# The first 25 microseconds of a grouped-query attention backward: K's load first, q and grad_out by ACT's queue, zero matmuls and an early exponential

## The chip, the cores and the metric

The kernel runs on one core of one Trainium2 chip. The metric is the device time in microseconds; the time before is the median of three runs. One further execution is taken with the hardware profiler, and all views of the profile come from it.

## The reference

Attention with 32 query heads on 4 key/value heads, 4 query positions and 2048 keys, for 32 batches, all in bf16; the kernel returns the output and the gradients of q, k and v for a given grad_out.

```python
B, Hq, Hkv, Sq, Sk, D = 32, 32, 4, 4, 2048, 128
k = jnp.repeat(k, rep, axis=1)
v = jnp.repeat(v, rep, axis=1)
scores = jnp.einsum("bhqd,bhkd->bhqk", q, k) * D ** -0.5
p = softmax(scores)
out = jnp.einsum("bhqk,bhkd->bhqd", p, v)
_out, _vjp = jax.vjp(forward, q, k, v)
return (_out, *_vjp(grad_out))
```

## The kernel before

A batch has 32 x 4 = 128 query rows, one for each partition, 32 for each key/value head. Its K and V are 2 MB each and lie in SBUF as 128 partitions x 4 heads x 16 chunks x 128; a load is four transfers, one for each head (lines 153 and 159), issued by SP. K has three buffers, V two. q and grad_out of four batches come together, by two transfers in GROUP (line 141): 128 partitions x 4 batches x 128 elements, so in runs of 256 bytes. Batch 0's pair is issued by SP inside LK(0), ahead of K; the later pairs are issued by POOL.

The work of a batch is cut into pieces with short names. QDT transposes q and grad_out on PE into one PSUM bank, and DVE copies both to SBUF as qdt (lines 170 and 172). KT0 to KT7 and VT0 to VT7 (function turned) each transpose eight 128 x 128 blocks of K or V on PE (line 180) and have DVE copy the bank (line 182); a piece with an even number needs heads 0 and 1, one with an odd number heads 2 and 3. Sa and Sb are the two halves of the scores: Sa needs KT0 to KT3, Sb KT4 to KT7, both need qdt; DVE takes the maximum of each (line 210) and forms negb (line 213). EXa and EXb are ACT's exponentials (line 221). NRM adds the two row sums (ls, line 236), takes the reciprocal, and POOL scales grad_out and q by it (line 230) into block pairs dop and qp, which are set to zero at the start (line 117). ETa and ETb transpose the exponentials back, O is the output, dP the gradient of the scores (line 349), dST its transpose, dQ, dV and dK the results; dV and dK are cast from PSUM by ACT (line 310) and stored by POOL (line 132), in the tail by SP.

The order in which every engine gets its instructions is written out by hand: HEAD names the pieces of the first iterations ("KT4@0" is piece KT4 of batch 0), STEADY those of one iteration, TAIL those of the last. Each engine runs its share of that order one after the other, and a piece that waits holds up what stands behind it on its engine. PSUM's eight banks are given out by the class Banks in the same order: the bank or pair that has been free longest. Both the scores' halves take two banks, a transposed piece one.

## Time and profile before

| | |
|---|---|
| runs, device us | 685.06, 686.15, 687.32 (median 686.15) |
| the profiled execution: its own time / its span | 682.75 / 680.5 us |
| busy share of the span | PE 92%, PEld 66%, DVE 87%, ACT 83%, POOL 38% |
| moved by transfers | 274.45 MB, mean 403 GB/s |
| granted clock of TensorE | 0.998 |
| K quarter loads, issue to landing, median | 14.5 us |

A busy share is an average over the whole span. PE is matrix work, PEld the loading of its weights, which overlaps; DVE, ACT and POOL are the other compute engines; SPq stands for SP's queue of transfer issues. In the views by time, a row has its start, its length, the engine, the line and the tiles, and in brackets how long the engine was idle before it and what it waited for. In the table by stretches, each engine's busy time in that stretch is followed by its number of instructions; the last three columns are the granted clock, the mean busy share of the 16 transfer engines, and what they moved in GB/s. A wait for several marks is put down in the profile to the one that came last, and where that one had long been there, it was another.

### The profile page before, as it was taken

What the parts mean: (1) busy time and instruction counts of PE and PEld (TensorE: products, weight loads), DVE (VectorE), ACT (ScalarE), POOL (GpSimd) and SP (SyncE); (2) the same over time, 40 slices, a digit from 0 to 9 for tenths busy, and PEclk for the clock granted to TensorE, in tenths of its full rate; (3) what the DMA queues carried; (4) which work ended last, traced back from release to release, by engine and by line L of the source; (5) the groups of instructions that cost most, each with busy time, mean ns of one, the idle gap of its engine ahead of it and who ended that gap; (6) DMA issues with size and microseconds to landing.
All of it is one profiled execution on the core that took longest, in us unless ns stands there. A gap on an engine that the chain in (4) does not pass through costs nothing.

```text
span 680.5 us, 27999 instructions
## 1 busy us (share of the span) xinstructions
PE 623.7 (92%) x12352; PEld 449.1 (66%) x12352; DVE 594.5 (87%) x1003; ACT 563.3 (83%) x666; POOL 259.6 (38%) x436
## 2 busy tenths in 40 slices
PE   5899999999999999988999999899999999899984
PEld 4577766667776667765667766577666677566652
DVE  4999999899899889889888889789898898898895
ACT  0599898898888888888988888888888888896885
POOL 1254243534424454432535324353244542344310
PEclk9999999999999999999999999999999999999999
DMA  8989999999999999999999999999999999999998
GB/s 326 406 293 400 416 417 411 416 413 416 416 414 417 412 417 415 416 416 415 416 416 414 416 414 417 414 411 416 414 417 398 409 414 416 415 401 406 370 368 317
DMA packets 76483, 274.45 MB, mean 403 GB/s; under 512 B 8579, under 2 KB 8651, under 8 KB 76361
## 3 DMA queue, kind: packets, MB, share of 16 engines
q1 hardware_dynamic: 42185, 145.11, 53.2%
q0 software_dynamic: 34176, 127.55, 46.6%
q8 instruction: 96, 1.57, 0.8%
q14 instruction: 26, 0.21, 0.1%
HBM read 136.31 MB, written 136.31 MB: 401 GB/s over the span
## 4 chain that ended last, share of the span: by engine, by line
PE 53%; DMA 36%; DVE 4%; ACT 3%; issue 2%; SPq 1%; POOL 0%; ACTq 0%; DVEq 0%; POOLq 0%
DMA k_sb<-in_k_dram 35%; PE banks L180 22%; PE banks L306 14%; PE banks L263 8%; PE banks L197 5%; PE banks L247 5%; ACT dv L310 2%; DVE kt L182 1%; DMA v_sb<-in_v_dram 1%; SPq L153 1%; DVE dk L310 1%; DVE m L210 1%; PE banks L170 1%; DVE ds L349 1%; DVE vt L182 0%
## 5 line engine op out<-in xcount | busy, mean ns | idle before, releaser
L310 ACT CAST dv<-banks 128x1024 bf16<-128x1024 f32 x254 | 244.4, 1025 | 47.7 <-PE banks L306 47.1
L310 ACT CAST dk<-banks 128x1024 bf16<-128x1024 f32 x251 | 246.0, 1022 | 29.9 <-PE banks L306 26.9
L182 DVE COPY kt<-banks 128x1024 bf16<-128x1024 bf16 x256 | 165.1, 680 | 9.9 <-PE banks L180 9.8
L182 DVE COPY vt<-banks 128x1024 bf16<-128x1024 bf16 x256 | 166.4, 680 | 2.6 <-PE banks L180 2.0
L180 PE MATMUL banks<-ident,k_sb 128*128 128x128 bf16 x2048 | 148.0, 221 | 18.5 <-DMA k_sb<-in_k_dram 13.3
L230 POOL TENSOR_SCALAR dop<-do_sb,rinv 32x128 bf16<-32x128 bf16 x124 | 74.2, 598 | 220.6 <-PE banks L306 125.2
L180 PE MATMUL banks<-ident,v_sb 128*128 128x128 bf16 x2048 | 143.5, 219 | 12.4 <-ACT dv L310 8.8
L180 PEld LDWEIGHTS <-k_sb 128*128 128x128 bf16 x2048 | 120.7, 99 | 48.4 <-issue 31.8
L180 PEld LDWEIGHTS <-v_sb 128*128 128x128 bf16 x2048 | 121.3, 98 | 28.2 <-issue 26.2
L306 PE MATMUL banks<-dop,e 64*128 64x256 bf16 x1024 | 97.6, 273 | 7.0 <-issue 4.3
L349 DVE SCALAR_TENSOR_TENSOR ds<-banks,delta,e 128x1024 bf16<-128x1024 f32 x64 | 82.0, 1283 | 17.1 <-PE banks L197 17.0
L306 PE MATMUL banks<-qp,ds 64*128 64x256 bf16 x1024 | 87.0, 272 | 2.6 <-DVE dk L310 1.1
L132 POOL DMA_DIRECT2D out_dram<-dv x46 | 32.5, 708 | 139.9 <-ACT dv L310 133.5
L230 POOL TENSOR_SCALAR qp<-q_sb,srinv 32x128 bf16<-32x128 bf16 x128 | 77.9, 609 | 10.7
L221 ACT ACTIVATE e<-banks,negb 128x1024 bf16<-128x1024 f32 x64 | 70.7, 1111 | 11.4 <-DVE negb L213 11.4
L210 DVE TENSOR_REDUCE m<-banks 128x1 f32<-128x1024 f32 x64 | 75.2, 1215 | 1.7 <-PE banks L197 1.5
L306 PEld LDWEIGHTS <-e 64*128 64x128 bf16 x1024 | 34.0, 94 | 52.9 <-issue 36.6
L249 DVE COPY et<-banks 128x1024 bf16<-128x1024 bf16 x64 | 41.4, 685 | 27.1 <-PE banks L247 27.0
L306 PEld LDWEIGHTS <-ds 64*128 64x128 bf16 x1024 | 40.8, 94 | 30.8 <-ACT dv L310 12.6
L249 DVE COPY dst<-banks 128x1024 bf16<-128x1024 bf16 x64 | 43.4, 679 | 0.0
L197 PE MATMUL banks<-vt,qdt 128*32 128x512 bf16 x512 | 41.3, 384 | 1.8 <-issue 1.6
L197 PE MATMUL banks<-kt,qdt 128*32 128x512 bf16 x512 | 39.6, 384 | 0.7 <-DVE vt L182 0.3
(40 smaller groups left out, 460.1 us busy)
## 6 DMA issues: line engine op xcount, KB each, us to landing
k_sb<-in_k_dram SPq DMA_DIRECT2D x128, 512.0 KB, 14.5
v_sb<-in_v_dram SPq DMA_DIRECT2D x128, 512.0 KB, 20.5
out_dram<-dk POOLq DMA_DIRECT2D x29, 2048.0 KB, 23.4
out_dram<-dv POOLq DMA_DIRECT2D x22, 2048.0 KB, 27.5
out_dram<-dv POOLq DMA_DIRECT2D x7, 1440.0 KB, 27.2
out_dram<-dk SPq DMA_DIRECT2D x2, 2048.0 KB, 10.3
out_dram<-dv POOLq DMA_DIRECT2D x7, 512.0 KB, 20.4
out_dram<-dv SPq DMA_DIRECT2D x1, 2048.0 KB, 12.0
```

Of the source, the lines that this page charges most:

```text
L180: nc.tensor.transpose(out=ps[:, 4 * hh + j, :], in_=S[which][:, 2 * (i % 2) + hh, 4 * (i // 2) + j, :], identity=ident[:])
L182: nc.vector.tensor_copy(out=S[f"{which}t{i}"][:], in_=ps)
L197: nc.tensor.matmul(ps[G * h:G * h + G, a, :], lhsT=S["qdt"][:, col, G * h:G * h + G], rhs=xt[:, 4 * (h % 2):4 * (h % 2) + 4, :].rearrange( ...
L210: nc.vector.reduce_max(out=S["m"][:, i:i + 1], in_=S[f"s{i}"][1], axis=AX.X)
L221: nc.scalar.activation(out=S[f"e{i}"][:], in_=ps, func=ACT.Exp, bias=S["negb"][:], scale=scale, accum_out=S["l"][:, i:i + 1],)
L230: engine.tensor_scalar(out=t[r, h % 2, :], in0=src[r, :], scalar1=by[r, :], scalar2=None, op0=ALU.mult)
L247: nc.tensor.transpose(out=ps[:, u, :], in_=S[f"{src}{i}"][:, P * u:P * u + P], identity=ident[:])
L249: nc.vector.tensor_copy(out=S[f"{name}{i}"][:], in_=ps)
L263: nc.tensor.matmul(ps[G * h:G * h + G, :], lhsT=S[f"{xt}{c // 8}"][:, c % 8, G * h:G * h + G], rhs=S[kv][:, h, c, :], start=(c == 0), stop ...
L306: nc.tensor.matmul(ps[:, a, :, c, :], lhsT=S[f"{x}{i // 4}"][r, u:u + P], rhs=S[y][r, :, :], start=True, stop=True, tile_position=(2 * G * ...
L310: copy(out=S[name][:, :, 2 * i:2 * i + 2, :].rearrange("p h c d -> p h (c d)"), in_=banks.ap(t).rearrange("p a (j w) -> p (a j) w", j=2),)
L349: nc.vector.scalar_tensor_tensor(out=S[f"ds{i}"][:], in0=ps, scalar=S["delta"][:], in1=S[f"e{i}"][:], op0=ALU.subtract, op1=ALU.mult,)
```

## The change

Batch 0's q and grad_out are issued by ACT in place of SP, so that SP's first transfer is K's first quarter. Behind these two issues, ACT takes one exponential of a single column of the identity, and with it the load of the exponential's table. On PE, 16 matrix products of the identity with the zeroed pair dop (256 columns, into one bank that is given back unread) stand ahead of everything else. Batch 0's pieces get another order: KT4 stands ahead of QDT, KT1 ahead of KT5 and KT7, and VT2 behind Sa and Sb. KT5 and KT7 of batch 0 are copied out of PSUM by ACT in place of DVE.

```diff
 HEAD = """
-LK@0 LV@0 QDT@0 KT4@0 KT6@0 KT2@0 KT0@0 KT3@0 KT5@0 KT1@0 KT7@0 LK@1 LV@1 VT2@0 Sa@0 Sb@0 VT5@0 VT3@0 EXb@0 VT4@0 EXa@0 VT0@0 QDT@1 KT4@1
+LK@0 LV@0 WARM@0 KT4@0 QDT@0 KT6@0 KT2@0 KT0@0 KT3@0 KT1@0 KT5a@0 KT7a@0 LK@1 LV@1 Sa@0 Sb@0 VT2@0 VT5@0 VT3@0 EXb@0 VT4@0 EXa@0 VT0@0 QDT@1 KT4@1
...
+WARM_MATMULS = 16
...
         if b == 0:
-            GROUP(0, nc.sync)
+            GROUP(0, nc.scalar)
+
+            first = sm_pool.tile([P, 1], FP32, name="first")
+            nc.scalar.activation(out=first[:], in_=ident[:, 0:1], func=ACT.Exp)
...
+    def WARM(b):
+
+        t = banks.take(1)
+        for _ in range(WARM_MATMULS):
+            nc.tensor.matmul(
+                banks.ap(t)[:, 0, 0:2 * D], lhsT=ident[:], rhs=pairs["dop", 0][:].rearrange("p a d -> p (a d)"), start=True, stop=True,
+            )
+        banks.give(t)
+
-    def turned(S, which, pool, i):
+    def turned(S, which, pool, i, copy=nc.vector.tensor_copy):
...
-        nc.vector.tensor_copy(out=S[f"{which}t{i}"][:], in_=ps)
+        copy(out=S[f"{which}t{i}"][:], in_=ps)
...
-    def KT(b, i):
-        turned(st[b], "k", kt_pool, i)
+    def KT(b, i, copy=nc.vector.tensor_copy):
+        turned(st[b], "k", kt_pool, i, copy)
...
+        table[f"KT{i}a"] = lambda b, i=i: KT(b, i, nc.scalar.copy)
```

More of the change, by code (lines that the diff above doesn't have):

```diff
@@ L352, in dP @@
         banks.give(t)
-    table = {"LK": LK, "LV": LV, "QDT": QDT, "O": O, "dQ": dQ, "NRM": NRM}
+    table = {"LK": LK, "LV": LV, "QDT": QDT, "O": O, "dQ": dQ, "NRM": NRM, "WARM": WARM}
     for i, c in enumerate("ab"):
```

## The prediction

> **What bounds the kernel now.** I read the whole-run bandwidth first, then the chain of waits, then a table by stretches of the first 65 us, then the first 25 us in order of time.

> ```profile
> span 680.5 us, 27999 instructions
> GB/s 326 406 293 400 416 417 411 416 413 416 416 414 417 412 417 415 416 416 415 416 416 414 416 414 417 414 411 416 414 417 398 409 414 416 415 401 406 370 368 317
> PE 53%; DMA 36%; DVE 4%; ACT 3%; issue 2%; SPq 1%; POOL 0%; ACTq 0%; DVEq 0%; POOLq 0%
> ```

> Each slice is 17 us. From the fourth to the thirty-seventh the transfers move some 415 GB/s almost without a break, and 274.45 MB at that rate are 661 of the 680.5 us: the run is a transfer stream with a poor start and a compute tail. The chain puts 53% on PE and only 36% on DMA, but the PE share lies before 260 us, where the engines are nearly full as well; the rate says that the stream has no room to catch up. The first and the third slice are what a head edit can touch. Stretch by stretch (us; busy time of PE, PEld, DVE, ACT, POOL; clock; DMA share; GB/s):

> ```profile
> 15.00:20.00 5.00, 3.38 (x51) 2.57 (x44) 4.96 (x8) 1.86 (x2) 0.00 (x0) 1.00 1.02 405
> 32.00:34.00 2.00, 2.00 (x32) 0.90 (x31) 2.00 (x4) 2.00 (x4) 0.00 (x0) 1.00 1.03 416
> 34.00:36.00 2.00, 1.49 (x28) 1.10 (x21) 1.96 (x3) 1.97 (x3) 0.64 (x1) 1.00 0.57 225
> 42.00:44.00 2.00, 2.00 (x42) 1.73 (x35) 1.18 (x4) 1.95 (x4) 1.17 (x2) 1.00 0.75 211
> 58.00:60.00 2.00, 1.99 (x33) 1.76 (x32) 2.00 (x5) 1.54 (x3) 0.00 (x0) 1.00 1.03 422
> ```

> Until 34 us the stream is full with the loads of batches 0 to 2. Then it runs at half rate until about 48 us, because what comes next waits for compute: the first dv store is issued at 35.36 us, K of batch 3 at 42.13, V of batch 3 at 47.23. Summed over 34 to 54 us, 5.98 MB move where 415 GB/s would move 8.3: 5.6 us of stream time are lost. So what makes batch 0's compute earlier or later by x moves these issues by x, and the end with them, since the stream is full behind them.

> The head in order of time (start, length, engine):

> ```profile
> 0.73 0.42 SPq L141 DMA_DIRECT2D q_sb<-in_q_dram  x1
> 1.75 1.92 SPq L153 DMA_DIRECT2D k_sb<-in_k_dram  x4
> 4.33 0.29 PE L170 MATMUL banks<-ident,do_sb 128*128 128x128 bf16 x1 [0.97 <-DMA do_sb<-in_grad_out_dram]
> 8.31 5.60 PE L180 MATMUL banks<-ident,k_sb 128*128 128x128 bf16 x60 [0.66 <-DMA k_sb<-in_k_dram]
> 9.81 0.69 DVE L182 COPY kt<-banks 128x1024 bf16<-128x1024 bf16 x1 [0.16 <-PE banks L180]
> 15.98 1.74 PE L180 MATMUL banks<-ident,v_sb 128*128 128x128 bf16 x28 [0.22 <-DMA v_sb<-in_v_dram]
> 17.96 2.47 DVE L182 COPY vt<-banks 128x1024 bf16<-128x1024 bf16 x4
> 18.13 1.28 ACT L221 ACT_TABLE_LOAD   x1 [18.13 <-DVE negb L213]
> 23.20 0.15 DVE L236 TENSOR_TENSOR ls<-l 128x1 f32<-128x1 f32 x1
> ```

> q and grad_out are in by 4.33, K's second quarter by 8.30, V's last quarter by 15.98. DVE works nearly without a gap from 8.95 to 23.20, where it has the row sums (ls); POOL then scales grad_out and dV can start. I use the start of ls as the head's mark: the chain of waits goes through it.

> **The parts of the change and their cost.**

> K first. The first 256-byte packet of q starts at 2.06 us, the first K packet at 3.25, so K starts about 1.2 us earlier. Gain at K's second quarter, before other effects: 1.2 us.

> q and grad_out on ACT's queue. They are 1024 packets of 256 B in the trace, 64 for each of 16 transfer engines at 18 ns; K and V are 1024 packets of 4096 B, also 64 for each engine, at 159 ns. Before, one queue held them in a row. Now two queues are full together, and what matters is how an engine shares itself. The trace has one stretch for this: from 54 to 56 us, POOL's stores and SP's loads both waiting, 102 and 103 packets of 4096 B were started. That is turn for turn, but equal sizes can't tell turns by packet from turns by bytes. By bytes, 256 KB land beside the first 256 KB of K, by about 5 us. By packets, grad_out's last packet has turn 64, together with V's last: 15.98 - 1.2 + 64 x 0.018 = 15.9 us. If ACT's issue is 0.42 us ahead of SP's (one issue, row above), 22 of its packets pass alone and the last has turn 42: V's second quarter less a little, 11.9 us. The nearest row for a small load beside a full queue is POOL's:

> ```profile
> v_sb<-in_v_dram SPq DMA_DIRECT2D x128, 512.0 KB, 20.5
> q_sb<-in_q_dram POOLq DMA_DIRECT2D x7, 128.0 KB, 22.9
> q_sb<-in_q_dram SPq DMA_DIRECT2D x1, 128.0 KB, 2.3
> ```

> Alone it takes 2.3 us, beside others no less than a load four times its size (some of it behind stores in its own queue). That is nearer to turns by packet; I take the middle of 11.9 and 15.9, so 13.9.

> [...]

> Order. QDT of batch 0 now stands behind KT4 and ahead of the seven other K pieces on PE, whose instructions run in order, and it needs grad_out. KT4 is done at about 7.8; then KT6 to KT7, the scores, and on DVE everything from the qdt copy on, wait for 13.9 where QDT waited only to 4.33 before. From grad_out's landing: 0.29 for two transposes, four pieces at the pace of a PE that has idled (DVE got the first at 8.95, 9.81, 10.66: 0.85 each) 3.4, then KT3 and KT1 leave DVE at 5.1. ACT takes KT5 and KT7 behind that: its copy of a bf16 bank is not in the trace, between DVE's 0.69 and the exponential's 1.11; I take the f32 cast's 1.02, so 6.7. Sb 0.6, its maximum 1.17, negb 0.2: 8.7. Then five V pieces (VT2 now stands behind the maxima) at 0.68, qdt 0.28, four K pieces of batch 1 2.72: ls at 15.2 behind the landing, 29.1 us, against 23.20: **+5.9**. At 11.9 it is +3.9, at 15.9 +7.9; it breaks even at 8.0.

> Zero matmuls: 16 of 256 columns. At 0.106 for 128 columns (0.85 for eight) 3.4 us, at L306's 273 ns 4.4; from the identity's 1.55 they end by 6.0, ahead of K's second quarter (8.30 - 1.2 + 16 x 0.018 = 7.4). They cost nothing while K is that late. What they could win is the 0.16 of each cold piece, at most 5 x 0.16 = 0.8; with PE idle from 7.8 to 13.9 I take none. [...]

> One exponential ahead: the table load's 1.28 goes to ACT's idle time before 18 us. It is off the path: from negb to ls DVE has 6.4 us of copies, the two exponentials take 2.3. Bounds: 0, and -1.28 if they led. I take 0. KT5 and KT7 on ACT take 2 x 0.69 from DVE; that is in the sum.

> Transfers behind: the build's waits have K of batch 1 wait for grad_out's completion mark, so SP issues it at 13.9 and not at 7.01. Its loads have 1 to 3 us of idle stream behind V, but batch 1's K is needed only at 24 or later, and the gap from 34 us covers the rest.

> **Sum.** 682.75 (the profiled execution's own time) + 5.9 = 688.7. The runs' median, 686.15, is 3.4 above that execution; on it the forecast is **692.0**, its own range 690.0 to 694.1.

> **Rivals.**
> 1. Shared by bytes, the far side: grad_out lands by 5, no stall. K pieces leave DVE by 12.3, negb is there at 15.4. But V's last quarter still lands at 15.98, since as many bytes go ahead of it; then four V pieces, qdt, four K pieces: 16.6 + 2.7 + 0.3 + 2.7 = 22.3, -0.9: 685.2. For it: nothing but the lack of a row with unequal packets. Against: POOL's row.
> 2. No stall, and the exponential leads, not DVE: it starts at 15.5 and not at 19.42, -3.9: 682.2. For it: PE waited 0.8 us for an exponential's bank. Against: DVE's 4.96 busy of 5.00.
> 3. A half stall: the landing at 8 to 9, as if ACT's queue had most of its packets ahead: 0 to +1, 686.7. Against: both engines leave the same barrier, and SP's first issue is at 0.73.

> **Chances.** Forecast 0.54, rival 1 0.17, rival 2 0.21, rival 3 0.08. A difference of under 0.3%, 2.1 us, is no change here. Forecast: all slower. Rival 1: same, with 0.03 of it faster. Rival 2: faster. Rival 3: half and half same and slower. So faster 0.24, same 0.18, slower 0.58. The range reaches from rival 2, a little cut, to the late end: 683.0 to 694.5.

> **What would show it.** Right: QDT's grad_out transpose at 12 to 16 us with PE idle from about 8, waiting on do_sb; ls near 29; the first dv store near 41 and K of batch 3 near 48; the later slices again near 415 GB/s. Wrong: grad_out in by 6 us, KT6 right behind KT4; ls at 22.3 would be rival 1. If ls is late and the end is not, the step from the head to the stream is wrong.

## The result and the profile after

| | before | after |
|---|---|---|
| runs, device us: median (range), 5 each | 685.06 (682.80 to 687.32) | 691.19 (688.47 to 691.52) |
| ratio, 95% interval | | 1.0074 (1.0049 to 1.0099) |
| profiled execution: its own time / span | 682.75 / 680.5 | 688.47 / 686.3 |
| mean granted clock of that execution | 0.998 | 0.993 |
| ls of batch 0 / first dv store / K of batch 3 issued | 23.20 / 35.36 / 42.13 | 23.75 / 37.47 / 44.24 |

The changed kernel is slower by 0.7% in this comparison, 691.19 us where 692.0 was forecast. An unchanged repeat, below, gave 1.0026 (0.9997 to 1.0055), an interval that just reaches 1. So the direction is likely, and the size lies between the two. But the way there was not the forecast one. Three executions that took over 1.5% longer than the fastest of their kernel (697.14, 696.45 and 697.61 us) stand in the medians and ranges below, but not in the ratios, nor in the fit of the last section. From the page of the changed kernel, the span, the bandwidth in 40 slices and the chain by engine:

```profile
span 686.3 us, 28036 instructions
GB/s 346 371 248 402 417 416 386 417 412 418 415 418 415 414 415 418 416 416 413 416 412 415 415 415 415 414 416 414 411 417 398 414 413 417 417 407 401 350 348 300
PE 74%; DMA 14%; issue 4%; DVE 3%; ACT 2%; SPq 1%; ACTq 0%; DVEq 0%
```

Six slices are clearly poorer: the second (371 for 406), the third (248 for 293), the seventh (386 for 411) and the last three (350, 348 and 300 for 370, 368 and 317). The first is richer (346 for 326): K's first packet starts at 1.75 us where it was 3.01. So there is not one loss at the head, but several along the run. The head of the changed kernel in order of time (start, length, engine, line, tiles; in brackets the idle time before and its releaser). All times here count from the profile's zero; the times of packets and of the clock in the prediction and the expectations (2.06, 3.25, 12.9, 14.4) lie 0.24 us later, which leaves the differences between them as they are.

```profile
0.72 0.46 ACTq L142 DMA_DIRECT2D q_sb<-in_q_dram  x1
0.73 1.98 SPq L157 DMA_DIRECT2D k_sb<-in_k_dram  x4
1.61 3.60 PE L183 MATMUL banks<-dop,ident 128*128 128x256 bf16 x16 [1.61 <-POOL ident masks.py:199]
1.77 1.28 ACT L151 ACT_TABLE_LOAD   x1 [1.77 <-issue]
6.25 0.61 PE L193 MATMUL banks<-ident,k_sb 128*128 128x128 bf16 x4 [0.61 <-DMA k_sb<-in_k_dram]
...
8.96 1.75 SPq L157 DMA_DIRECT2D k_sb<-in_k_dram  x4
8.99 0.29 PE L174 MATMUL banks<-ident,do_sb 128*128 128x128 bf16 x1 [2.03 <-DMA do_sb<-in_grad_out_dram]
...
14.38 1.93 ACT L195 COPY kt<-banks 128x1024 bf16<-128x1024 bf16 x2 [11.11 <-PE banks L193]
18.17 3.07 DVE L195 COPY vt<-banks 128x1024 bf16<-128x1024 bf16 x5
23.75 0.15 DVE L249 TENSOR_TENSOR ls<-l 128x1 f32<-128x1 f32 x1
25.71 0.27 PE L319 MATMUL banks<-dop,e 64*128 64x256 bf16 x1 [0.98 <-POOL dop L243]
27.08 0.38 PE L319 MATMUL banks<-dop,e 64*128 64x256 bf16 x3 [1.10 <-DVE vt L195]
27.38 1.56 PE L276 MATMUL banks<-v_sb,et 128*32 128x128 bf16 x64
```

PE does wait for grad_out behind KT4, as forecast, but until 8.96 and not 13.9, and K of batch 1 is issued at that very moment. ls comes 0.55 us later than in the profile before. From ls to the first dv store it takes 13.72 us where it took 12.16, and the stretches (busy time of PE, PEld, DVE, ACT, POOL; clock; DMA share; GB/s) show why:

```profile
25.00:30.00 5.00, 3.19 (x80) 1.75 (x79) 3.33 (x8) 1.48 (x2) 4.35 (x8) 0.78 0.84 328
30.00:32.00 2.00, 2.00 (x28) 1.14 (x20) 1.49 (x2) 1.50 (x2) 0.14 (x1) 0.70 0.96 330
36.00:38.00 2.00, 1.49 (x27) 1.00 (x20) 2.00 (x2) 2.00 (x3) 0.53 (x1) 1.00 0.03 12
58.00:60.00 2.00, 2.00 (x37) 1.89 (x34) 1.97 (x5) 1.59 (x4) 0.29 (x1) 1.00 1.03 414
```

The granted clock falls to 0.78 and 0.70: TensorE was at half clock for 3.41 us from 27.8 on by the trace's clock records. The same 64 products of O took 1.56 us here and 1.08 in the profile before, where the first dv store followed at 35.36:

```profile
26.74 1.08 PE L263 MATMUL banks<-v_sb,et 128*32 128x128 bf16 x64
35.36 2.33 POOL L132 DMA_DIRECT2D out_dram<-dv  x3 [5.95 <-ACT dv L310]
```

(The column for the clock shows 1.00 until a trace's first clock record. That PE is at half clock ahead of it is read from the rows: four transposes of K take 0.61 us there, and 0.40 in the repeat below, where the records show full clock from 4.8 us on; and eight take 0.85 there, as in the repeat's recorded half-clock stretch from 8.2 to 15.0.) In the changed kernel the stream then all but stops (12 GB/s) until the first dv store at 37.47, and it is full again at 58 us.

When each kernel had moved as many bytes as the other, by the records of all packets, the changed kernel was 0.9 us ahead at 10 us, 0.7 behind at 34, 2.1 behind at 38, 2.5 from 60 to 100, some 3.4 from 120 to 640 and 5.8 at the end. That is the ledger of these two executions: ls 0.55, half clock 1.56, a poor spell between 100 and 120 us 1.0, the tail about 2.3, and 0.4 in between. The tail's term is not the change's: a second profile of the kernel before (before_again, below) loses 2.0 us on the first one from 600 us to its end, and the changed kernel loses 2.5 there. Against that second profile the changed kernel is 3.8 us behind at 60 us and 3.4 at the end.

### The profile page after: what moved, and what is told of

Its sections match the earlier page's. It is cut to its first block, busy times and chain, and to the rows that moved or that the text cites. A ratio compares the mean times of both kernels' runs of the same rounds, so it can differ in the third digit from the quotient of the medians.

```text
span 686.3 us, 28036 instructions
## 1 busy us (share of the span) xinstructions
PE 631.7 (92%) x12368; PEld 455.6 (66%) x12368; DVE 593.7 (87%) x1001; ACT 565.4 (82%) x669; POOL 259.4 (38%) x436
## 2 busy tenths in 40 slices
DMA packets 76483, 274.45 MB, mean 400 GB/s; under 512 B 8579, under 2 KB 8651, under 8 KB 76361
## 4 chain that ended last, share of the span: by engine, by line
PE 74%; DMA 14%; issue 4%; DVE 3%; ACT 2%; SPq 1%; ACTq 0%; DVEq 0%
PE banks L193 31%; PE banks L319 19%; DMA k_sb<-in_k_dram 12%; PE banks L276 9%; PE banks L210 8%; PE banks L260 7%; ACT dv L323 2%; DMA do_sb<-in_grad_out_dram 1%; DVE vt L195 1%; PE banks L174 1%; DMA v_sb<-in_v_dram 1%; DVE dk L323 1%; SPq L157 1%; DVE kt L195 0%; DVE m L223 0%
## 5 line engine op out<-in xcount | busy, mean ns | idle before, releaser
L193 PEld LDWEIGHTS <-k_sb 128*128 128x128 bf16 x2048 | 123.1, 100 | 42.1 <-issue 35.7
L193 PEld LDWEIGHTS <-v_sb 128*128 128x128 bf16 x2048 | 121.4, 98 | 31.6 <-issue 29.1
L362 DVE SCALAR_TENSOR_TENSOR ds<-banks,delta,e 128x1024 bf16<-128x1024 f32 x64 | 82.1, 1284 | 21.3 <-PE banks L210 20.5
L210 PE MATMUL banks<-vt,qdt 128*32 128x512 bf16 x512 | 42.7, 388 | 3.9 <-issue 3.7
## 6 DMA issues: line engine op xcount, KB each, us to landing
k_sb<-in_k_dram SPq DMA_DIRECT2D x128, 512.0 KB, 13.5
v_sb<-in_v_dram SPq DMA_DIRECT2D x128, 512.0 KB, 19.9
out_dram<-dv POOLq DMA_DIRECT2D x22, 2048.0 KB, 22.5
out_dram<-dv POOLq DMA_DIRECT2D x7, 512.0 KB, 15.5
```

The source lines that it names most:

```text
L193: nc.tensor.transpose(out=ps[:, 4 * hh + j, :], in_=S[which][:, 2 * (i % 2) + hh, 4 * (i // 2) + j, :], identity=ident[:])
L210: nc.tensor.matmul(ps[G * h:G * h + G, a, :], lhsT=S["qdt"][:, col, G * h:G * h + G], rhs=xt[:, 4 * (h % 2):4 * (h % 2) + 4, :].rearrange( ...
L362: nc.vector.scalar_tensor_tensor(out=S[f"ds{i}"][:], in0=ps, scalar=S["delta"][:], in1=S[f"e{i}"][:], op0=ALU.subtract, op1=ALU.mult,)
```

## The experiments

All ratios are to the kernel before, run beside it on the same chip; its medians there were 687.0, 686.1 and 685.69 us (35, 27 and 29 runs). "Landing" is when the transposition of grad_out starts on PE, with PE's idle time ahead of it where grad_out was what it waited for (where there was none, grad_out had landed earlier); the last three columns are from one profiled execution each. In the diffs, ... stands for lines that are left out, and the long lines of HEAD are shown in part.

| kernel | median (range, runs) | ratio, 95% | landing (PE's wait) | ls | first dv store |
|---|---|---|---|---|---|
| before, first profile | | | 4.33 (0.97) | 23.20 | 35.36 |
| after, first profile | 691.19 (688.47 to 691.52, 5) | 1.0074 (1.0049 to 1.0099) | 8.99 (2.03) | 23.75 | 37.47 |
| again | 689.33 (685.57 to 697.14, 12) | 1.0026 (0.9997 to 1.0055) | 9.83 (3.27) | 24.61 | 38.33 |
| qdt_late | 685.57 (683.42 to 687.91, 12) | 0.9987 (0.9964 to 1.0010) | 11.16 (none) | 20.98 | 33.23 |
| no_warm | 687.39 (684.40 to 691.52, 12) | 1.0011 (0.9984 to 1.0037) | 8.61 (1.80) | 22.66 | 36.32 |
| sync_first | 686.54 (683.92 to 692.12, 12) | 1.0001 (0.9978 to 1.0024) | 7.98 (none) | 21.91 | 35.67 |
| fill | 688.87 (685.73 to 692.85, 8) | 1.0056 (1.0027 to 1.0084) | 7.31 (0.53) | 21.38 | 33.64 |
| late_fill | 686.25 (684.36 to 689.96, 12) | 1.0008 (0.9986 to 1.0029) | 10.88 (none) | 21.05 | 33.69 |
| split | 685.99 (683.36 to 688.12, 12) | 1.0001 (0.9984 to 1.0019) | 6.83 (0.19) | 21.09 | 33.35 |
| pairs | 692.80 (688.67 to 695.90, 4) | 1.0092 (1.0048 to 1.0136) | 12.16 (5.31) | 26.98 | 40.74 |
| before_again | 685.93 (682.17 to 696.45, 12) | 0.9998 (0.9971 to 1.0024) | 3.92 | 21.72 | 33.87 |
| split_o | 684.80 (682.63 to 686.84, 12) | 0.9983 (0.9965 to 1.0001) | 6.83 (0.30) | 20.98 | 32.46 |
| preload | 689.99 (one run) | | 4.25 | 22.30 | 35.91 |
| copies | 683.89 (682.63 to 687.17, 10) | 0.9976 (0.9954 to 0.9998) | 4.10 | 22.27 | 34.43 |

### The changed kernel and the kernel before, once more

No edit, for the spread of both profiles. The expectations set two readings against each other: by theory C the loss is made of stretches at half clock, by rival H of the wait for grad_out alone.

> The changed kernel once more, for its spread and for the clock of each run. Theory C (clock): the loss beside the kernel before is made mostly of stretches of 3.4 us in which PE runs at half clock, each worth about 1.6 us where PE sets the pace, and not of the head's order; then the ten runs of both kernels line up by their mean granted clock (0.998 goes with 683, 0.987 with 691), and the profile here has ls near 23.7 and a half-clock stretch between 25 and 32 us again. Rival H (head): the loss is in the wait for grad_out alone; then the time stays at 690 to 691.5 whatever the clock is.

> The kernel before once more, for a second profile of it and for what the comparison gives of two equal kernels: a ratio of 1.000 with an interval that has 1. Nine profiles of kernels with a changed head have a spell of slow transfers between 102 and 118 us (1.0 to 1.9 us lost), and the one profile of the kernel before has none. If the spell goes with the changed head it is absent here again; if the profile of before was a lucky one, it is here too, and the mean clock is nearer to the runs' 0.992 than to 0.998.

The repeat of the changed kernel took 689.33 us, ratio 1.0026, its interval just reaching 1: less than in the first comparison, but the two intervals share 1.0049 to 1.0055. Its head is like the first one's, a little later:

```profile
9.83 0.29 PE L174 MATMUL banks<-ident,do_sb 128*128 128x128 bf16 x1 [3.27 <-DMA do_sb<-in_grad_out_dram]
24.61 0.15 DVE L249 TENSOR_TENSOR ls<-l 128x1 f32<-128x1 f32 x1
38.33 2.33 POOL L133 DMA_DIRECT2D out_dram<-dv  x3 [7.34 <-ACT dv L323]
```

From ls to the store it is 13.72 us again, with a half-clock stretch from 28.7 to 32.1.

The kernel before gave this:

```profile
8.83 0.69 DVE L182 COPY kt<-banks 128x1024 bf16<-128x1024 bf16 x1 [0.16 <-PE banks L180]
9.69 3.76 DVE L182 COPY kt<-banks 128x1024 bf16<-128x1024 bf16 x6 [0.16 <-PE banks L180]
21.72 0.15 DVE L236 TENSOR_TENSOR ls<-l 128x1 f32<-128x1 f32 x1
33.87 2.34 POOL L132 DMA_DIRECT2D out_dram<-dv  x3 [5.95 <-ACT dv L310]
```

ls is 1.48 us earlier than in its first profile, with not a word of the program changed. The copies of the K pieces show where from: K's second quarter was in at 7.34 and not 8.31, and after two pieces (0.16 us of idle ahead of each: PE's pieces come 0.85 apart and a copy takes 0.69) DVE goes through without gaps; in the first profile there were four such gaps ahead of copies. PE came to full clock at 10.0 us here and at 12.7 there. So one profile tells ls to about 1.5 us only, and a difference of that size between two heads is no finding by itself.

### Where QDT stands, and where grad_out comes from

qdt_late moves QDT of batch 0 right ahead of the scores, so that nothing waits for grad_out behind KT4. sync_first gives q and grad_out back to SP's queue ahead of K and keeps all else. no_warm takes the zero matmuls out.

```diff
-LK@0 LV@0 WARM@0 KT4@0 QDT@0 KT6@0 KT2@0 KT0@0 KT3@0 KT1@0 KT5a@0 KT7a@0 LK@1 LV@1 Sa@0 Sb@0 VT2@0
+LK@0 LV@0 WARM@0 KT4@0 KT6@0 KT2@0 KT0@0 KT3@0 KT1@0 KT5a@0 KT7a@0 LK@1 LV@1 QDT@0 Sa@0 Sb@0 VT2@0
```

> QDT of batch 0 stands right ahead of Sa, so that no K piece waits for grad_out. Rival H: ls comes at 22.0 in place of 23.75, and the time falls to that of the kernel before or under it (683 to 685). Theory C: ls comes at about 22 as well, but the time stays within 2 us of the changed kernel's (689 to 691), unless the half-clock stretches are gone; the mean clock tells which.

```diff
-            GROUP(0, nc.scalar)
+            GROUP(0, nc.sync)
```

> q and grad_out are issued by SP ahead of K again; the rest of the change stays. grad_out lands at 4.3, K's second quarter at 8.3. Rival H: no wait on grad_out, ls at 22.5 to 23, time 684 to 685.5. Theory C: the same ls, but a time that goes with the clock: 685 at 0.997, 690 at 0.988.

```diff
-LK@0 LV@0 WARM@0 KT4@0 QDT@0 KT6@0
+LK@0 LV@0 KT4@0 QDT@0 KT6@0
```

> The zero matmuls are left out. In the profile of the changed kernel PE comes to full clock at 14.4 us in spite of them, against 12.9 before without them, so both theories expect no gain lost: ls within 0.3 of 23.75, the time within 1 us of the changed kernel's. If the zero matmuls shift when the clock drops (a part of theory C), the number of half-clock stretches falls and the time goes to 686 or so. If they did warm PE, ls comes 0.6 later.

Without the wait the loss is gone: qdt_late 0.9987, sync_first 1.0001. Against the repeat's 1.0026 alone that would be little; it is the whole table that speaks: the kernels with PE waiting half a microsecond or more for grad_out behind KT4 have 1.0011 to 1.0092, those with no such wait or 0.3 us at most 0.9983 to 1.0008. qdt_late's head in order of time:

```profile
6.93 2.48 DVE L195 COPY kt<-banks 128x1024 bf16<-128x1024 bf16 x4 [6.93 <-PE banks L193]
11.16 0.22 PE L174 MATMUL banks<-ident,do_sb 128*128 128x128 bf16 x1
14.65 1.74 PE L193 MATMUL banks<-ident,v_sb 128*128 128x128 bf16 x28 [0.64 <-DMA v_sb<-in_v_dram]
20.98 0.15 DVE L249 TENSOR_TENSOR ls<-l 128x1 f32<-128x1 f32 x1
33.23 2.33 POOL L133 DMA_DIRECT2D out_dram<-dv  x3 [5.95 <-ACT dv L323]
```

Four K copies run without a gap from 6.93, PE then waits for K's and V's transfers (2.6 and 0.6 us) and no longer for grad_out, and ls comes 2.8 us before that of the changed kernel. PE was at full clock from 5.9 us, with the same zero matmuls ahead; in the changed kernel it was so only from 14.1. The repeat shows the wait's part in this: PE was at full clock from 4.8 to 8.2 us there, and with the wait it fell back to half until 15.0. The wait thus cost twice there: 3.27 us of PE's time, and a PE at half clock behind it (four copies with 0.16 of idle ahead, as in the first profile before). qdt_late takes away the wait and the half-clock stretch at 28 us together, so it does not part C from H. sync_first has no wait for grad_out, but K's pieces are later there, with the issues put back ahead of K (its second quarter is in at 7.69 and not 6.25): ls 21.91, below the 22.5 that was expected. no_warm was not slower than the repeat beside it: 687.39 against 689.33. So the zero matmuls show no gain in this kernel; the intervals overlap too far to call them harmful. Its ls of 22.66 lies outside the 0.3 us around 23.75 that was expected. Whether they help where no wait follows was not tried: no kernel with QDT late leaves them out.

### How two queues share the engines

split puts the two loads on SP's queue between K's second and third quarter. pairs loads batch 0's K in two transfers of 1 MB in place of four of 512 KB, with q and grad_out on ACT's queue as in the changed kernel.

```diff
-            GROUP(0, nc.scalar)
...
         for h in range(NH):
+            if b == 0 and h == 2:
+                GROUP(0, nc.sync)
             nc.sync.dma_start(out=S["k"][:, h].rearrange("p c d -> p (c d)"), in_=k_v[b, h])
...
```

> q and grad_out on SP's own queue between K's second and third quarter, the rest as changed. In one queue they are not mixed with K: grad_out lands at 7.2 to 7.8, PE waits for it under 1 us behind KT4, and ls comes at 21.8 to 22.3. By the head alone (rival H) the time is 1.5 to 2.5 under the changed kernel's; by theory C it is 1.5 less and goes with the clock, 685.5 to 688.

```diff
-        for h in range(NH):
-            nc.sync.dma_start(out=S["k"][:, h].rearrange("p c d -> p (c d)"), in_=k_v[b, h])
+        for h in range(0, NH, 2 if b == 0 else 1):
+            w = 2 if b == 0 else 1
+            nc.sync.dma_start(out=S["k"][:, h:h + w].rearrange("p h c d -> p h (c d)"), in_=k_v[b, h:h + w].rearrange("h p x -> p h x"))
```

> The changed kernel with batch 0's K in two transfers of 1 MB in place of four of 512 KB; SP's packets stay 4096 bytes. It asks what an engine's turn is. Turns by transfer (an engine ends one queue's transfer, then takes the other's): q's packets come in a burst behind K's first MB, grad_out's behind its second, at 7.6 to 8.2 us, and the last straggle in at 10 or later, where they landed at 8.6 to 9.8 before; ls is 0.5 to 1.5 later. Turns of a fixed size: the bursts stay at 3.5 to 4.5 and 5.0 to 6.5 us and the landing at 8.6 to 9.8. Turns by single packets: no bursts, landing near 14.

In split PE waits 0.19 us for grad_out and ls is 21.09. In pairs grad_out is in 3.2 us later than in the changed kernel, and ls and the first store move by the same 3.2 and 3.3:

```profile
6.84 0.69 DVE L196 COPY kt<-banks 128x1024 bf16<-128x1024 bf16 x1 [6.84 <-PE banks L194]
12.16 0.29 PE L175 MATMUL banks<-ident,do_sb 128*128 128x128 bf16 x1 [5.31 <-DMA do_sb<-in_grad_out_dram]
12.49 0.29 DVE L177 COPY qdt<-banks 128x256 bf16<-128x256 bf16 x1 [4.96 <-PE banks L175]
26.98 0.15 DVE L250 TENSOR_TENSOR ls<-l 128x1 f32<-128x1 f32 x1
40.74 2.34 POOL L133 DMA_DIRECT2D out_dram<-dv  x3 [7.45 <-ACT dv L324]
```

The packets started in each half microsecond, counted from the traces (q and grad_out: 256 B; K and V: 4096 B), tell how the engines were shared:

```
from us     changed kernel: 256 B  4096 B     pairs: 256 B  4096 B
3.0                           39      45                25      48
3.5                          370      13                48      48
4.0                          103      46                48      48
4.5                            0      51                48      47
5.0                          163      28               221      24
5.5                          245      25               143      41
6.0                           28      42                43      43
7.0                           24      52                44      45
8.0                            7      50                60      45
9.0                            0      51                43      44
10.0                           0      51                50      48
11.0                           0      49                19      47
```

In pairs the two queues went packet for packet, some 45 to 45, as long as K's megabyte lasted: between 6.2 and 9.4 us a large packet started 2 to 4 ns before a small one's end 316 times, where other distances of that width have some 50, so the turns there were of single packets. In the half microsecond in which the first megabyte ended (at 5.4), 221 small packets went beside 24 large ones, and then it was turn for turn again until 11.3. In the changed kernel there are two such bursts, one for q and one for grad_out, where K's first and second quarter end (3.75 and 5.43). The reading of these two traces: inside a transfer of SP's queue one packet of each (45 and 45 in pairs), and at its end ACT's queue ran nearly alone for a moment (370 beside 13, 245 beside 25, 221 beside 24). That fits the direction of pairs, which has fewer ends and a later landing, but not every end: where the second megabyte of pairs ends, at 8.4 us, there is hardly a burst (60 beside 45). Why not stays open; more and smaller transfers were not tried.

### The half-clock stretch at 25 to 32 us

fill puts 20 products of the identity with the still zero pair dop of batch 1 (one bank, unread) between VT1 and dV7 of batch 0, where PE waits 0.98 and 1.10 us for POOL's scaling and a V copy. late_fill has the same on top of qdt_late.

```diff
-NRM@0 ETb@0 ETa@0 VT7@0 KT3@1 VT6@0 VT1@0 dV7@0 O@0
+NRM@0 ETb@0 ETa@0 VT7@0 KT3@1 VT6@0 VT1@0 FILL@0 dV7@0 O@0
...
+        for _ in range(20):
+            nc.tensor.matmul(
+                banks.ap(t)[:, 0, 0:2 * D], lhsT=ident[:], rhs=pairs["dop", 1][:].rearrange("p a d -> p (a d)"), start=True, stop=True,
+            )
```

> The changed kernel with 20 more zero matmuls on PE between VT1 and dV7 of batch 0, where PE waited 0.98 and 1.10 us for POOL's dop and the clock then fell to half. They take 2.2 us at full clock, about the wait, so that ls and what hangs on it stay where they were (23.7 to 24.7). Theory C (the half clock near 28 us comes of PE's idle time while it waits for dop): no half-clock stretch between 24 and 33 us, the first dv store 1.5 us earlier against ls than in the changed kernel (13.0 behind ls in place of 13.7, as before: 35.36 against 23.20 is 12.2), and the time 1.5 us lower, 687 to 688. Rival (the clock falls for another reason, by chance): the stretch is there as often as before, and the time is the changed kernel's plus up to 0.5.

> QDT ahead of Sa, and the same 20 zero matmuls. No stretch fell between 24 and 33 us with QDT late, so both theories expect the time of that kernel, 684.5 to 686, with ls at 21 and a mean clock of 0.995 or more. If the stretch had been missed there by luck alone, the matmuls make its absence sure, and the spread of the runs gets smaller.

In place fill does what it should, though its ls is 21.38 where 23.7 to 24.7 was expected: grad_out landed earlier, at 7.31, which the added products behind it can't have caused. The same stretch of the changed kernel (first line: changed kernel, in a fence of its own) and of fill:

```profile
26.00:30.00 4.00, 2.92 (x79) 1.66 (x78) 2.33 (x6) 1.48 (x2) 3.51 (x7) 0.72 0.79 307
```

```profile
26.00:30.00 4.00, 4.00 (x68) 2.24 (x60) 3.70 (x7) 3.41 (x5) 1.53 (x3) 1.00 1.03 410
```

PE is busy throughout, the clock stays at 1.00, and ls to the first store is 12.26 us in place of 13.72. But the time, 688.87, is no better than the repeat's 689.33, above the 687 to 688 that I had expected. In fill's own chain of waits between 40 and 64 us stands a new item of about the size won:

```profile
43.07 1.60 issue
```

There PE waited for nothing that the profile shows. Whether the 20 added instructions bring that gap or it fell there by chance, one profile does not tell. So the price of the half-clock stretch is shown in place (1.5 us at the first store) and not in the time at the end. The other profiles bear the price out: from ls to the first store it is 13.61 to 13.76 us in the six with such a stretch behind ls, and 12.15 to 12.26 in the six without one that keep the order dV7, O, late_fill apart (12.64). fill also shows that an early head is no early end: its first store came 1.7 us ahead of that of the first profile before, and by bytes moved it was 0.1 behind that profile at 60 us and 1.7 behind at 600. late_fill had no stretch to remove, since qdt_late has none in its profile, and it took 686.25 against 685.57: no gain.

### The other parts alone, and the best version

preload is the kernel before with the early exponential only. copies is the kernel before with KT5 and KT7 copied by ACT, KT1 ahead of them and VT2 behind the scores. split_o is split with O of batch 0 ahead of dV7, for the wait on POOL.

```diff
+            first = sm_pool.tile([P, 1], FP32, name="first")
+            nc.scalar.activation(out=first[:], in_=ident[:, 0:1], func=ACT.Exp)
```

> The kernel before with the early exponential alone. The table load of 1.28 us leaves the place between negb and the first exponential. By the prediction's step DVE sets ls, and the load is worth 0; the wait row gives at most 0.8 (PE waited so long for an exponential's bank ahead of batch 1's K pieces). ls at 22.4 to 23.2, against 23.20.

```diff
-LK@0 LV@0 QDT@0 KT4@0 KT6@0 KT2@0 KT0@0 KT3@0 KT5@0 KT1@0 KT7@0 LK@1 LV@1 VT2@0 Sa@0 Sb@0 VT5@0
+LK@0 LV@0 QDT@0 KT4@0 KT6@0 KT2@0 KT0@0 KT3@0 KT1@0 KT5a@0 KT7a@0 LK@1 LV@1 Sa@0 Sb@0 VT2@0 VT5@0
...
```

> The kernel before with KT5 and KT7 of batch 0 copied by ACT and with the changed order of KT1 and VT2 alone. ACT's first instruction is now a copy, so the table load also leaves the path. DVE is relieved of 2 x 0.69: ls at 21.9 to 22.3, as in sync_first (21.91), which has this edit, the zero matmuls and K pieces ahead of QDT. If the zero matmuls were what helped there, ls stays at 23. Time 0.5 to 1.5 us under the kernel before.

```diff
-VT7@0 KT3@1 VT6@0 VT1@0 dV7@0 O@0 dV5@0
+VT7@0 KT3@1 VT6@0 VT1@0 O@0 dV7@0 dV5@0
```

> The split kernel with O of batch 0 ahead of its dV7, so that PE has 64 matmuls to do while it waits for POOL's dop. Both theories: ls at 21 as in split, the first dv store not later than 33.4, no half-clock stretch between 22 and 33 us; the time 685 to 686, at best 1 us under split's. Worse than split if O's late transposed exponentials hold up dV7.

copies is the only kernel whose interval lies below 1: 683.89 us, 0.9976 (0.9954 to 0.9998), 1.8 us under the median beside it, a little more than expected. Of twelve intervals one that misses 1 by so little can come by chance. Its head:

```profile
0.73 1.28 ACT L182 ACT_TABLE_LOAD   x1 [0.73 <-PEq L400]
12.90 1.93 ACT L182 COPY kt<-banks 128x1024 bf16<-128x1024 bf16 x2 [10.89 <-PE banks L180]
16.57 0.21 DVE L213 TENSOR_SCALAR negb<-m 128x1 f32<-128x1 f32 x1
16.87 1.11 ACT L221 ACTIVATE e<-banks,negb 128x1024 bf16<-128x1024 f32 x1 [2.05 <-PE banks L180]
22.27 0.15 DVE L236 TENSOR_TENSOR ls<-l 128x1 f32<-128x1 f32 x1
```

negb comes 1.26 us earlier than in the first profile before, the exponential follows without a table load (that stands at 0.73, ahead of ACT's first copy, with no exponential added for it), and ls is 0.93 earlier. With full clock from 11.4 us in place of 12.7 a part of that may be the clock's; what can be said rests on the ten runs. Against the second profile before, ls (22.27 for 21.72) and the first store (34.43 for 33.87) are later and not earlier. preload has ls at 22.30, but a half-clock stretch from 26.3 to 29.7 and two later ones, and its single time, 689.99, says nothing about the part. split_o has the earliest first store of all, 32.46, and 0.9983 (0.9965 to 1.0001): an improvement is likely there, but not established.

### What stays open

Heads that are 1.5 to 2 us earlier than that of the first profile before (qdt_late, split, late_fill) end at its time and not under it. Against the second profile before, whose first store came at 33.87, they are only 0.2 to 0.6 us early. By bytes moved, qdt_late is 1.6 us ahead of the first profile from 80 to 100 us, and 0.5 ahead at 120. All ten profiles of kernels built on the changed one lose in the same place. The first line is the kernel before, the second the changed kernel, each in its own fence:

```profile
100.00:120.00 20.00, 19.22 (x388) 13.78 (x378) 18.15 (x32) 17.70 (x22) 7.18 (x12) 1.00 1.02 413
```

```profile
100.00:120.00 20.00, 19.43 (x393) 14.16 (x391) 18.52 (x33) 18.01 (x22) 7.18 (x12) 1.00 1.02 391
```

The transfer engines are about as busy as ever (share 0.98 to 1.02) and move less: 369 to 398 GB/s in the ten, 407 to 413 in before, before_again, copies and preload. At 20 us of 413, 391 is 1.1 us of stream time and 376 (split and sync_first) 1.8. It is not ACT's queue (sync_first and split have none of it), not the zero matmuls (no_warm), and neither the exponential alone (preload) nor ACT's copies (copies) bring it. The order with KT4 ahead of QDT is common to the ten; it was not tried by itself, nor were the exponential and the copies together. The slow packets are mostly those of POOL's queue: from 98 to 122 us 80 packets of 4096 B took over 200 ns in the changed kernel, 68 of them POOL's, against 22 and 18 in the kernel before, and what they took beyond 159 ns is 1.1 us of all 16 engines' time against 0.2. What slows them I don't know.

## Why the prediction was right and where it was wrong

**What bounds the kernel.** Right. Behind the head the stream is full at 414 GB/s at 58 us, and the gap from 34 us moves with the first dv store: store and K of batch 3 both came 2.11 us later than in the profile before (37.47 and 44.24). Passing the head's delay to the end one for one held in pairs: its first store is 5.4 us behind that of the first profile before and 6.9 behind the second; the median is 6.7 over that of the kernel before beside it. It did not hold for early heads: fill's lead was gone by 60 us, qdt_late's 1.6 us shrank to 0.5 by 120.

**The wait behind KT4.** Right in its mechanism. QDT waited with PE idle, DVE's qdt copy and all K pieces behind it, and K of batch 1 was issued at grad_out's landing. Moving QDT alone (qdt_late) took the ratio from 1.0026 to 0.9987, about 2.7 us by the ratios and 3.8 in the medians.

**The landing: the step that failed.** "I take the middle of 11.9 and 15.9, so 13.9." It was 8.96, 9.8 in the repeat, 8.6 in no_warm and 7.3 in fill with the same two queues: below the lower bound, which supposed turns by single packet all the way, with 22 of ACT's packets ahead of K. None went ahead: ACT's first packet started at 3.05 us, 2.3 behind its issue, and K's first at 1.75. Turns by single packet are what pairs shows inside K's transfers (some 45 beside 45), but where K's first and second quarter end ACT's queue ran nearly alone, 370 small packets in the half microsecond from 3.5 and 408 in the microsecond from 5.0. The only case that held the bound of 11.9 was pairs (12.16), where K has two transfers for four. The row that I leaned on, POOL's 22.9 us for a small load, was a load behind stores in its own queue (the first issued at 50.60 us, 1.47 behind a dk store); it said less than I took from it. That landing is rival 3's, which I gave 0.08.

**From the landing to ls, 15.2.** Right: 14.76 in the changed kernel, 14.78 in the repeat, 14.82 in pairs. In no_warm it was 14.05 and in fill 14.07, where PE came to full clock earlier (12.3 and 11.0 us).

**The sum of +5.9.** The profiled execution came out +5.7, by other terms. The head gave 0.55 of it at ls against the first profile before, 2.0 to 2.9 against the second. The half-clock stretch gave 1.56, the spell at 100 to 120 us 1.0, and the tail about 2.3, most of which an unchanged execution of the kernel before loses on that first profile too. None of these three was in the sum. The forecast of 692.0 for a median of 691.19 is therefore a landing too late by 5 us and three terms not seen, which nearly cancel: that the number fits is luck, and the repeat, 1.8 us over the kernel before by its ratio, does not fit it. That the end would be late only as far as ls is late was wrong here.

**K first.** Forecast at 7.4 for the second quarter; 6.25 came, and 5.7 to 6.5 in the other kernels that begin with K. The kernel before itself has 8.31 and 7.34, so some 1 to 2 us were gained, and given back at grad_out.

**Zero matmuls at 0.** Right, so far as can be told: no_warm was no slower. That nothing would be won of the 0.8 with PE idle in the wait was the author's estimate; no trace of the kernel before shows what such a wait does to the clock. In the repeat the clock fell there: full from 4.8 to 8.2 us, with PE busy 0.96 us of these, then half to 15.0, with the wait (6.56 to 9.83) in between. In the first profile there was no full clock before 14.1 at all, with PE busy for 2.30 and 2.44 us of the two stretches of 3.41 us that hold the zero matmuls and KT4.

**The early exponential at 0, ACT's copies at 2 x 0.69 less on DVE.** The exponential's bound of -1.28 was the better end in the kernel before: PE's wait for the exponential's bank (0.78 us in both profiles) is gone in copies, which moves the table load too. ACT's copy took 0.97 us and not 1.02. These parts together are worth some 1.8 us (copies, interval 0.1 to 3.2); that the wait hid them in the changed kernel is likely, but not shown.

**The rivals.** Rival 1, sharing by bytes, is out by the counts in pairs (some 45 packets of 256 B beside 45 of 4096 B). Rival 2, no stall, became real in qdt_late; its gain of 3.9 us was 0.9 by the ratio.

## What to carry to other kernels

A small load with short runs that something soon needs should not be put on a second queue beside large loads without looking at how the packets take turns (grad_out was there at 8.99 us in place of 4.33, with K in larger transfers at 12.16); when it must be, let its user stand late in the order. A transfer moved off a queue is worth only what the first instruction behind its landing allows, so ask of every moved load which in-order engine stops for it, and whether its clock falls meanwhile, as PE's did in the repeat (half from 8.2 to 15.0 us). Test the parts one by one: here the two loads on ACT's queue with QDT behind them lost some 3 to 4 us, the zero matmuls showed nothing, and the plainest edit (two copies on an idle engine, with the order beside them) won some 1.8 us when left alone, if its interval is to be trusted. And take more than one profile of the kernel before: two of them, with no edit in between, had ls 1.48 us apart.

## What the hardware showed beyond that

Over 211 runs of these kernels, each taken against the mean of its own kernel in its own series, the time went with the mean granted clock: correlation -0.70, 0.52 us for each 0.001. One stretch of 3.41 us is 0.0025 of the run's mean, so some 1.3 us, near the 1.5 that it cost at the first store. Much of the spread between runs of one kernel may be of that kind; that it is the cause is not shown.
